# The tiles behind the tail phases of a cross network, multiplied in four 32-column strips instead of one 128-column block

## The chip, the cores and the metric

The kernel runs on one core of a Trainium2 chip. The metric is the time of one execution on the device in microseconds (us). A core has a matrix engine (TensorE; in the profile PE for its matmuls and PEld for its weight loads), VectorE (DVE), ScalarE (ACT), GpSimd (POOL), and SyncE (SP), which issues nearly all transfers here.

## The reference: six cross layers over 16384 rows

```
B, F, D, L = 16384, 26, 16, 6
Din = min(F * D, 1024)                      # 416
x = x0                                      # [16384, 416], bfloat16
for l in range(L):
    proj = jnp.einsum('bd,de->be', x, ws[l]) + bs[l]
    x = x0 * proj + x
return x
```

Each layer is a product of [16384, 416] with [416, 416], a bias, a multiplication with the first input and an addition of the layer's own input.

## The kernel before: groups, jobs, tiles, tails and row products

**Layout.** The 416 features are three full blocks of 128 and a tail of 32. Features stand on partitions and batch rows run along the free dimension, so a weight block is the stationary operand and x the moving one. The batch is cut into 8 groups of 2048 rows, a group into `NJ` = 4 chunks of `CH` = 512, which is one PSUM bank of f32. A job (g, l) is one layer of one group; the list `order` (lines 217 to 221) mixes jobs of several groups so that a layer's inputs are done long before the next layer wants them.

**Tiles.** A job has three tiles, i = 0, 1, 2: 128 output features for all four chunks, in four PSUM banks. `full` (line 467) issues the 12 matmuls over the three full blocks of input features, t = 0, 1, 2, each time for chunks 0 to 3, with 128x128 weights and 512 moving columns (line 479). `rows32` (line 486) adds what the 32 tail features contribute: four matmuls whose weights have 32 rows and 128 columns, each in another strip of 32 array rows (line 500), or, with `small`, sixteen with 32x32 weights (line 494). `evacuate` (line 378) then empties the banks: ScalarE adds the bias (line 406), VectorE multiplies with x0 (line 415) and adds x (line 420).

**Tails.** The 32 output features of the tail would fill a quarter of the array. `tails` (line 506) takes several jobs at once, each with one bank, in which the four chunks lie on the four strips of 32 partitions. It issues per job four 32x32 matmuls for the tail inputs (line 512) and then twelve matmuls with 128x32 weights for the full blocks (line 521): the four chunks of one t are at four column positions of the array, 0, 32, 64 and 96. `evacuate_tail` follows with ScalarE (line 446) and VectorE (lines 448 and 450). There are 14 tail phases: one with a single job at the start, called from `first_job`, and 13 in the list `items`, with 2, 3 or mostly 4 jobs.

**Order.** The program is one list per engine. `Program` works out the semaphore waits from reads and writes; nothing is reordered. PSUM banks are dealt from a ring of eight by `take`. Tiles come in pairs: the first (mode "FR") runs `full`, then `rows32`; the second ("RF") runs `rows32`, then `full`, so that the row products of two tiles stand together. A lone tile ahead of a tail phase has mode "F1": `full`, then the sixteen small row products, behind which the small products of `tails` follow at once. The tile straight behind a tail phase is always the first of a pair, so the array's form goes 32x32, 128x32 (tails), 128x128 (the tile's `full`), 32x128 (row products), 128x128, and so on. The first two tiles of the list have their own function, `two_tiles` (line 812), behind the tail phase of `first_job`: the matmuls of t = 0 for tiles 0 and 1, then t = 1 and 2 for tile 0, the row products of both, and t = 1 and 2 of tile 1.

**A side rule.** In the jobs (1, 2), (2, 1) and (3, 0), `full` splits matmuls into two of 256 columns each until a budget of 63 splits is used up (`HALVES`, `halves`).

**Text of this document.** "Set" is used for the four 128x32 matmuls of one t that stand at the four column positions, and "switch" for a change of the weights' form (rows x columns) from one matmul to the next.

Of the kernel before, what the change touches and what calls it, by code (L numbers as in the profile page):

```python
# [3 lines left out]
P = 128  # L4
CH = 512
T32 = 32
# [15 lines left out]
class Program:  # L22
# [12 lines left out]
    def add(self, eng, fn, reads=(), writes=(), lane=None, batch=None, hold=False, release=False):  # L35
        op = Op(eng, fn, lane, batch)
        deps = {}
        if eng == "pool":
            writes = list(writes) + ["pool"]
        for t in reads:  # L40
            w = self.writer.get(t)
            if w is not None:
                deps[id(w)] = (w, True)
        for t in writes:
            w = self.writer.get(t)
            if w is not None:
                deps[id(w)] = (w, True)
            for r in self.readers.get(t, ()):
                if id(r) not in deps:
                    deps[id(r)] = (r, False)  # L50
        for d, raw in deps.values():
            if d.lane is None and d.eng == eng and lane is None and (eng == "pe" or not raw):
                continue
            op.deps.append(d)
        for t in reads:
            self.readers.setdefault(t, []).append(op)
        for t in writes:
            self.writer[t] = op
            self.readers[t] = []
        if eng == "dve":  # L60
            if hold:
                self.flush()
                self.held = op
            else:
                self.queue[eng].append(op)
                if release:
                    self.flush()
        else:
            self.queue[eng].append(op)
        if lane is not None:  # L70
            batches = self.lanes.setdefault(lane, [])
            if not batches or batches[-1][0] != batch:
                batches.append((batch, []))
            batches[-1][1].append(op)
        return op
# [123 lines left out]
def bass_standalone__cross_network_dcn__recsys_kernel(  # L199
# [8 lines left out]
    NT = 3  # L208
    NJ = 4
# [15 lines left out]
    n = 0  # L225
# [7 lines left out]
    wm = [nc.alloc_sbuf_tensor(f"wm_{l}", [P, NT, D], BF16) for l in range(L)]  # L233
# [14 lines left out]
    psum = nc.alloc_psum_tensor("ps", [P, 8 * CH], FP32)  # L248

    pr = Program(nc)  # L250
    add = pr.add
# [16 lines left out]
    def bank(b, p0=0, p1=P, n=CH):  # L268
        return psum[p0:p1, b * CH:b * CH + n]
# [18 lines left out]
    def wm_tok(l, i):  # L288
        return ("wm", l) if i < 2 else ("wm", l, "rest")
# [58 lines left out]
    def x_src(g, l):  # L348

        if l == 0:  # L350
            s = slot(g)
            return lambda t, a, b: x0s[s][:, t * GC + a * CH:t * GC + b * CH], lambda t, j: x0_tok(s, t, j)
        s = xset[(g, l)]
        return lambda t, a, b: xs[s][:, t * GC + a * CH:t * GC + b * CH], lambda t, j: ("x", s, t, j)
# [109 lines left out]
    HALVES = ((1, 2), (2, 1), (3, 0))  # L464
    halves = [63]

    def full(g, l, i, banks, first, chunk_major, after_chunk=None, chunks=range(NJ), ts_=range(NT)):
        src, stok = x_src(g, l)
        ecols = slice(i * P, (i + 1) * P)
        seq = [(t, j) for j in chunks for t in ts_] if chunk_major else \  # L470
              [(t, j) for t in ts_ for j in chunks]
        for t, j in seq:
            n = 1
            if (g, l) in HALVES and halves[0] and t != (0 if first else NT - 1):
                halves[0] -= 1
                n = 2
            w = CH // n
            for k in range(n):
                add("pe", lambda h, t=t, j=j, k=k, w=w: h.matmul(  # L479
                    bank(banks[j])[:, k * w:(k + 1) * w], wm[l][:, t, ecols], src(t, j, j + 1)[:, k * w:(k + 1) * w],  # L480
                    start=(first and t == 0), stop=(not first and t == NT - 1)),
                    reads=[stok(t, j), wm_tok(l, i)], writes=[("ps", banks[j])])
            if after_chunk and t == NT - 1:
                after_chunk(j)

    def rows32(g, l, i, banks, first, small=False, inner=False):
        src, stok = x3_src(g, l)
        ecols = slice(i * P, (i + 1) * P)
        for j in range(NJ):
            r, q = quad(g, l, j)  # L490
            if small:
                for c in range(NJ):
                    o = slice(c * T32, (c + 1) * T32)
                    add("pe", lambda h, q=q, j=j, r=r, c=c, o=o: h.matmul(  # L494
                        psum[o, banks[j] * CH:(banks[j] + 1) * CH],
                        w3[l][q, i * P + c * T32:i * P + (c + 1) * T32], src[q, :],
                        start=first, stop=not first, tile_position=(r * T32, c * T32)),
                        reads=stok + [("w3", l, r)], writes=[("ps", banks[j])])
                continue
            add("pe", lambda h, q=q, j=j, r=r: h.matmul(  # L500
                bank(banks[j]), w3[l][q, ecols], src[q, :], start=first and not inner,
                stop=not first and not inner,
                tile_position=(r * T32, 0)),
                reads=stok + [("w3", l, r)], writes=[("ps", banks[j])])
# [39 lines left out]
    def load_nat(j, k0, k1):  # L544
# [6 lines left out]
        reads=["warm"], writes=["warm"])  # L551
# [117 lines left out]
    def job_banks():  # L669
        return take(NJ)  # L670
# [41 lines left out]
    def spread(eng):  # L712

        dst = ost[:, :, NT * P:D].rearrange("p (j k) f -> p j k f", j=NJ)
        sp_ = ot3[:, :, :].rearrange("p k (j f) -> p j k f", j=NJ)
        kw = dict(reads=["ot3"], writes=[("ost", NT, j) for j in range(NJ)])
        if eng == "act":
            add("act", lambda h: h.activation(dst, sp_, ACT_F.Copy), **kw)
        else:
            add(eng, lambda h: h.tensor_copy(dst, sp_), **kw)  # L720
# [23 lines left out]
    items = []  # L744
# [35 lines left out]
    def start_job(g, l):  # L780
        started.add((g, l))
        xset[(g, l + 1)] = free_x.pop(0)
        if (g, l) in W_LOAD:
            load_wm(W_LOAD[(g, l)], "sp")
            load_w3(W_LOAD[(g, l)], "sp")
        if (g, l) in G_LOAD:
            load_group(G_LOAD[(g, l)])
# [3 lines left out]
    def finish_tile(g, l, n=1):  # L791
        tiles_done[(g, l)] = tiles_done.get((g, l), 0) + n
        if tiles_done[(g, l)] == NT:
            done_with(g, l)
# [17 lines left out]
    def two_tiles(g, l):  # L812


        assert items[:2] == [("tile", (g, l), 0), ("tile", (g, l), 1)]
        bks = [job_banks(), job_banks()]
        for i in (0, 1):
            full(g, l, i, bks[i], True, False, ts_=[0])
        full(g, l, 0, bks[0], True, False, ts_=[1, 2])
        rows32(g, l, 0, bks[0], False)  # L820
        evacuate(g, l, 0, bks[0], list(range(NJ)), 2)
        finish_tile(g, l)
        rows32(g, l, 1, bks[1], False, inner=True)
        full(g, l, 1, bks[1], False, False, ts_=[1, 2])
        evacuate(g, l, 1, bks[1], list(range(NJ)), 2)
        finish_tile(g, l)
# [3 lines left out]
    for n, it in enumerate(items):  # L830
        if it[0] == "tails":
            tails(it[1])
            continue
        _, (g, l), i = it
        if (g, l) not in started:
            start_job(g, l)
        if n == 0:
            two_tiles(g, l)
            continue
        if n == 1:  # L840
            continue
        if mode[n] in ("FR", "F1"):
            banks = job_banks()
            full(g, l, i, banks, True, False)
            rows32(g, l, i, banks, False, mode[n] == "F1")
            evacuate(g, l, i, banks, list(range(NJ)), 2)
        else:
            banks = job_banks()
            rows32(g, l, i, banks, True)
            if n == len(items) - 1:  # L850
                full(g, l, i, banks, False, True, lambda j: evacuate(g, l, i, banks, [j], 1))
            else:
                full(g, l, i, banks, False, False)
                evacuate(g, l, i, banks, list(range(NJ)), 2)
        finish_tile(g, l)
        if (g, l) == (LAST, L - 2) and i < NT - 1:
            if i:
                spread("act")
            rest_turn(i)


    g, l = LAST, L - 1
    src, stok = x_src(g, l)
# [90 lines left out]
    bks = {0: bka, 1: [b0, b1, b2, a0], 2: [a1, a2, a3, b3], 3: [b0, b1, b2, a0]}  # L954
# [70 lines left out]
```

## Time and profile before

| What | Value |
|---|---|
| Median of 3 runs | 475.86 us (475.6 to 476.08) |
| Span of the profiled execution, first to last instruction | 474.4 us |
| Median less span (what lies around the span) | 1.46 us |
| Granted TensorE clock, mean of the span | 0.999 |
| PE busy; matmuls in the trace | 463.0 us (98%); 3354 |
| Weight loads in the trace | 3408 |
| DVE busy; ACT busy | 404.5 us (85%); 341.2 us (72%) |
| Matmuls of line 521 (tails, 128x32) | 564, 379 to 390 ns each |
| Matmuls of line 479 (full blocks, 128x128) | 1575 with 512 columns, 126 with 256 |

A matmul's duration in this profile is modelled from its issue to the end of its output, and matmuls overlap. The pace of the matrix engine is therefore read from the distance between the starts of neighbours, not from the durations. Some matmul records are missing (3354 of 3408; every matmul has its own weight load, and all the loads are there), so a distance that is longer by exactly one pace is a missing record and no pause. In the timeline view, a line has the start, the time until the last of its instructions ended, the engine, the line of the kernel, the operation with its tiles, the form and the count; what is in brackets is idle time of the engine ahead of it.

### The profile page before, as it was taken

The page shows a single profiled execution, that of the slowest core. Times are in us where ns is not written, and L with a number is a line of the kernel's source. Part 1 is how long each engine was busy: PE and PEld are TensorE (multiplying, and loading weights), DVE is VectorE, ACT ScalarE, POOL GpSimd, SP SyncE. Part 2 cuts the span into 40 slices and gives each one's busy share as a digit, 9 for nine tenths or more (in the row PEclk, how much of TensorE's full clock was granted, in tenths as well). Part 3 has the DMA queues.
Part 4 walks back from the last instruction along what each step waited for, and adds up shares of the span by engine and source line. Part 5 has one row for each costly group of instructions (what it writes and reads, how often), then busy time and mean ns, then how long its engine had stood idle before and what let it go on. Part 6 is the DMA issues. An engine that isn't in the chain of part 4 may idle for free.

```text
span 474.4 us, 8414 instructions
## 1 busy us (share of the span) xinstructions
PE 463.0 (98%) x3354; PEld 200.0 (42%) x3408; DVE 404.5 (85%) x700; ACT 341.2 (72%) x371; POOL 6.6 (1%) x15
## 2 busy tenths in 40 slices
PE   8999999999999999999999999999999999999996
PEld 5344444654444444444444444444444444444442
DVE  1888888888888888898889869988888888888897
ACT  4687777777777777777777777777777777777775
POOL 1000000000000000000000000000000000001000
PEclk9999999999999999999999999999999999999999
DMA  8996830730102388369319950880001039026999
GB/s 224 183 176 142 177 84 1 137 87 1 33 2 46 69 234 145 76 146 233 89 24 163 245 102 7 191 271 1 1 10 27 0 62 240 22 46 102 234 166 289
DMA packets 139052, 53.18 MB, mean 112 GB/s; under 512 B 112763, under 2 KB 138501, under 8 KB 139013
## 3 DMA queue, kind: packets, MB, share of 16 engines
q1 hardware_dynamic: 138856, 52.54, 50.0%
q8 instruction: 26, 0.43, 0.4%
q10 hardware_dynamic: 156, 0.11, 0.1%
q14 instruction: 14, 0.11, 0.1%
HBM read 5.97 MB, written 13.63 MB: 41 GB/s over the span
## 4 chain that ended last, share of the span: by engine, by line
PE 92%; DMA 2%; DVE 2%; ACT 2%; issue 1%; SPq 0%; DVEq 0%
PE ps L479 77%; PE ps L500 7%; PE ps L521 6%; ACT tw L406 2%; DMA wm<-in_ws_dram 1%; PE ps L494 1%; DVE x L940 1%; DMA x<-x 1%; DVE x L934 1%; PE ps L512 1%; DMA ot<-x 1%; DVE tw L415 0%; PE ps L600 0%; SPq L545 0%; DVE x L610 0%
## 5 line engine op out<-in xcount | busy, mean ns | idle before, releaser
L406 ACT ACTIVATE tw<-ps,bias 128x1024 bf16<-128x1024 f32 (+1 forms) x295 | 299.8, 1071 | 119.5 <-PE ps L500 81.1
L479 PE MATMUL ps<-x,wm 128*128 128x512 bf16 (+1 forms) x1701 | 372.1, 371 | 6.2 <-issue 3.7
L479 PEld LDWEIGHTS ps<-x,wm 128*128 128x128 bf16 x1755 | 165.1, 98 | 209.5 <-issue 28.2
L415 DVE TENSOR_TENSOR tw<-tw,x 128x1024 bf16<-128x1024 bf16 (+1 forms) x285 | 192.6, 683 | 51.9 <-ACT tw L406 51.5
L420 DVE TENSOR_TENSOR x<-tw,x 128x1024 bf16<-128x1024 bf16 (+1 forms) x285 | 182.5, 681 | 0.0
L500 PE MATMUL ps<-x,w 32*128 32x512 bf16 x512 | 39.2, 379 | 0.0
L521 PE MATMUL ps<-x,wm 128*32 128x512 bf16 x564 | 33.0, 380 | 0.0
L446 ACT ACTIVATE ts<-ps,bias 128x512 bf16<-128x512 f32 x47 | 28.8, 701 | 0.0
L450 DVE TENSOR_TENSOR x<-ts,x 128x512 bf16<-128x512 bf16 x47 | 18.6, 417 | 3.9 <-DMA x<-x 3.9
L521 PEld LDWEIGHTS ps<-x,wm 128*32 128x32 bf16 x564 | 13.8, 96 | 17.6 <-issue 5.3
L500 PEld LDWEIGHTS ps<-x,w 32*128 32x128 bf16 x512 | 7.8, 92 | 26.9 <-issue 26.4
L448 DVE TENSOR_TENSOR ts<-ts,x 128x512 bf16<-128x512 bf16 x47 | 18.6, 418 | 0.0
L720 POOL COPY ost<-ot 128x512 bf16<-128x512 bf16 x6 | 5.1, 854 | 422.2 <-DMA ot<-x 422.2
L876 PE MATMUL ps<-wm,x 128*128 128x416 bf16 x48 | 9.7, 340 | 0.0
L610 DVE COPY x<-ps 128x512 bf16<-128x512 bf16 x5 | 2.0, 423 | 8.9 <-PE ps L600 8.9
L928 ACT ACTIVATE x<-ps 128x416 bf16<-128x416 f32 x16 | 7.7, 517 | 2.1 <-PE ps L876 1.9
L612 ACT ACTIVATE x<-ps 128x512 bf16<-128x512 bf16 x7 | 3.8, 595 | 5.6 <-PE ps L600 5.6
L876 PEld LDWEIGHTS ps<-wm,x 128*128 128x128 bf16 x48 | 4.2, 98 | 4.4 <-issue 1.0
L512 PE MATMUL ps<-x,w 32*32 32x512 bf16 x188 | 5.9, 374 | 0.0
L494 PE MATMUL ps<-x,w 32*32 32x512 bf16 x208 | 5.6, 385 | 0.0
L940 DVE TENSOR_TENSOR x<-x,x 128x832 bf16<-128x832 bf16 (+1 forms) x9 | 4.7, 541 | 0.2
L934 DVE TENSOR_TENSOR x<-x,x 128x832 bf16<-128x832 bf16 (+1 forms) x10 | 4.8, 498 | 0.0
(40 smaller groups left out, 34.0 us busy)
## 6 DMA issues: line engine op xcount, KB each, us to landing
out_dram<-ost SPq DMA_DIRECT2D x6, 1664.0 KB, 7.0
x<-x SPq DMA_DIRECT2D x24, 96.0 KB, 2.1
x<-in_x_dram SPq DMA_DIRECT2D x8, 208.0 KB, 4.9
x<-in_x_dram SPq DMA_DIRECT2D x4, 416.0 KB, 8.4
out_dram<-ost SPq DMA_DIRECT2D x2, 832.0 KB, 5.5
wm<-in_ws_dram SPq DMA_DIRECT2D x5, 312.0 KB, 3.5
x<-x SPq DMA_DIRECT2D x22, 64.0 KB, 2.0
out_dram<-x SPq DMA_DIRECT2D x3, 416.0 KB, 4.4
```

The source lines that it names most:

```text
L406: add("act", lambda h, a=a, w=w, b0=b0: h.activation(tw[r][:, a * CH:(a + w) * CH], psum[:, b0 * CH:(b0 + w) * CH], ACT_F.Identity, bias=b ...
L415: add("dve", lambda h, a=a, e=e: h.tensor_tensor(tw[r][:, a * CH:e * CH], tw[r][:, a * CH:e * CH], x0s[s0][:, i * GC + a * CH:i * GC + e * ...
L420: add("dve", lambda h, a=a, e=e: h.tensor_tensor(xs[so][:, i * GC + a * CH:i * GC + e * CH], tw[r][:, a * CH:e * CH], src(i, a, e), ALU.ad ...
L446: add("act", lambda h: h.activation(ts[r][:, :], bank(b), ACT_F.Identity, bias=bias[:, 3, l:l + 1], scale=1.0), reads=[("ps", b), "bias"], ...
L448: add("dve", lambda h: h.tensor_tensor(ts[r][:, :], ts[r][:, :], x03, ALU.mult), reads=[("ts", r)] + tok0, writes=[("ts", r)], release=True)
L450: add("dve", lambda h: h.tensor_tensor(x3s[so][:, :], ts[r][:, :], res, ALU.add), reads=[("ts", r)] + rtok, writes=[("x3", so), ("x3", so, ...
L479: add("pe", lambda h, t=t, j=j, k=k, w=w: h.matmul(bank(banks[j])[:, k * w:(k + 1) * w], wm[l][:, t, ecols], src(t, j, j + 1)[:, k * w:(k ...
L494: add("pe", lambda h, q=q, j=j, r=r, c=c, o=o: h.matmul(psum[o, banks[j] * CH:(banks[j] + 1) * CH], w3[l][q, i * P + c * T32:i * P + (c + ...
L500: add("pe", lambda h, q=q, j=j, r=r: h.matmul(bank(banks[j]), w3[l][q, ecols], src[q, :], start=first and not inner, stop=not first and no ...
L512: add("pe", lambda h, l=l, b=b, s3=s3, ri=ri, qi=qi, ro=ro, qo=qo: h.matmul(psum[qo, b * CH:(b + 1) * CH], w3[l][qi, NT * P:D], s3[qi, :], ...
L521: add("pe", lambda h, t=t, j=j, src=src, l=l, b=b, ro=ro, qo=qo: h.matmul(psum[qo, b * CH:(b + 1) * CH], wm[l][:, t, NT * P:D], src(t, j, ...
L876: add("pe", lambda h, t=t: h.matmul(bank(b, n=D), xcol(t, j, kk), wm[l][:, t, :], start=(first and t == 0), stop=(not first and t == NT - 1)),
```

## The change

`full` gets a flag `columns`. With it, each 128x128 matmul becomes four matmuls with 128x32 weights, at column positions 0, 32, 64 and 96, which write the four strips of 32 partitions of the same bank and read the same 128x512 piece of x. The flag is set for every tile of mode "FR" or "F1" that follows a tail phase in the list, and in `two_tiles` for what stands ahead of the row products. The row products of these tiles, and all other tiles, stay as they are. The split into halves is passed over for a tile with the flag.

```diff
-    def full(g, l, i, banks, first, chunk_major, after_chunk=None, chunks=range(NJ), ts_=range(NT)):
+    def full(g, l, i, banks, first, chunk_major, after_chunk=None, chunks=range(NJ), ts_=range(NT), columns=False):
...
         for t, j in seq:
+            if columns:
+                for c in range(NJ):
+                    o = slice(c * T32, (c + 1) * T32)
+                    add("pe", lambda h, t=t, j=j, c=c, o=o: h.matmul(
+                        psum[o, banks[j] * CH:(banks[j] + 1) * CH],
+                        wm[l][:, t, i * P + c * T32:i * P + (c + 1) * T32], src(t, j, j + 1),
+                        start=(first and t == 0), stop=(not first and t == NT - 1), tile_position=(0, c * T32)),
+                        reads=[stok(t, j), wm_tok(l, i)], writes=[("ps", banks[j])])
+                continue
             n = 1
...
         for i in (0, 1):
-            full(g, l, i, bks[i], True, False, ts_=[0])
-        full(g, l, 0, bks[0], True, False, ts_=[1, 2])
+            full(g, l, i, bks[i], True, False, ts_=[0], columns=True)
+        full(g, l, 0, bks[0], True, False, ts_=[1, 2], columns=True)
...
             banks = job_banks()
-            full(g, l, i, banks, True, False)
+            full(g, l, i, banks, True, False, columns=items[n - 1][0] == "tails")
             rows32(g, l, i, banks, False, mode[n] == "F1")
```

Thirteen tiles of the list get 36 matmuls and 36 weight loads more each, and `two_tiles` gets 48 of each more.

## The prediction, on record before the run

> **What bounds the kernel now.** I read the page first, then the groups with their forms kept apart, then the timeline around one tail phase in ever narrower windows.
>
> ```profile
> span 474.4 us, 8414 instructions
> PE 463.0 (98%) x3354; PEld 200.0 (42%) x3408; DVE 404.5 (85%) x700; ACT 341.2 (72%) x371; POOL 6.6 (1%) x15
> ...
> PEclk9999999999999999999999999999999999999999
> ...
> PE 92%; DMA 2%; DVE 2%; ACT 2%; issue 1%; SPq 0%; DVEq 0%
> ```
>
> PE holds 92% of the chain that ended last and its clock is whole throughout, so time taken off PE's own list of work comes off the end, unless a wait takes its place. A busy share says nothing about the pace, so I look at starts. The groups with forms apart give what a narrow and a wide weight load cost:
>
> ```profile
> L479 PEld LDWEIGHTS ps<-x,wm 128*128 128x128 bf16 x1755 | 165.1, 98 | 209.5 <-issue 28.2 <-ACT ts L446 3.8 <-ACT bias L643 1.1
> L521 PE MATMUL ps<-x,wm 128*32 128x512 bf16 x564 | 33.0, 380 | 0.0
> L521 PEld LDWEIGHTS ps<-x,wm 128*32 128x32 bf16 x564 | 13.8, 96 | 17.6 <-issue 5.3
> ```
>
> One load takes 96 to 98 ns in either form. The timeline around the tail phase at 155 us (four jobs), one window wide:
>
> ```profile
> 154.68 0.43 PE L494 MATMUL ps<-x,w 32*32 32x512 bf16 x16
> 154.90 0.42 PE L512 MATMUL ps<-x,w 32*32 32x512 bf16 x16
> 155.22 2.12 ACT L406 ACTIVATE tw<-ps,bias 128x1024 bf16<-128x1024 f32 x2 [1.27 <-PE ps L494]
> 155.26 2.77 PE L521 MATMUL ps<-x,wm 128*32 128x512 bf16 x48
> 157.22 2.42 ACT L446 ACTIVATE ts<-ps,bias 128x512 bf16<-128x512 f32 x4
> 157.96 2.27 PEld L479 LDWEIGHTS ps<-x,wm 128*128 128x128 bf16 x12 [0.42 <-ACT ts L446]
> 158.19 2.54 PE L479 MATMUL ps<-x,wm 128*128 128x512 bf16 x11 [0.16 <-issue]
> 160.66 0.61 PE L500 MATMUL ps<-x,w 32*128 32x512 bf16 x8
> ```
>
> and in narrow windows, where single starts can be seen:
>
> ```profile
> 155.49 0.60 PE L521 MATMUL ps<-x,wm 128*32 128x512 bf16 x8
> ...
> 157.64 0.39 PE L521 MATMUL ps<-x,wm 128*32 128x512 bf16 x4
> ...
> 160.35 0.38 PE L479 MATMUL ps<-x,wm 128*128 128x512 bf16 x1
> ```
>
> The reader is to see three things. **The pace:** the second set of four starts at 155.49 and the twelfth at 157.64: ten steps in 2.15 us, 0.216 a set. Single 128x128 matmuls run at the same pace: from 158.19 to 160.35 there are ten steps, 2.16 us. So four narrow matmuls side by side cost what one wide one costs. **The switch:** from the tails' last set (157.64) to the first wide matmul, whose record is missing (12 loads, 11 matmuls; its load starts at 157.96), it is 0.32 and not 0.216. From the last wide matmul (160.35) to the first row product (160.66) it is 0.31. From a switch's first matmul or set to the second it is again some 0.01 more than the pace (158.19 less 157.96 is 0.23). So a switch costs 0.09 to 0.12 us, each way and between all the forms here. **Nobody waits:** between 154.68 and 160.66 PE has no other gap.
>
> **The change, part by part.**
>
> 1. *The switch behind the tails goes.* Before, the last set of the tails to the first row product: 160.66 - 157.64 = 3.02 us. After, twelve more sets follow at the pace, 12 x 0.216 = 2.59, and then the switch from a set of four to 32x128. That last step isn't in the trace. Nearest rows: 0.31 for wide to 32x128 (160.35 to 160.66), measured from a single matmul; 0.32 for a set of four to wide; 0.35 for a block of sixteen 32x32 to a set of four (154.90 to 155.26). I take 0.32, the same set on its way out. After: 2.59 + 0.32 = 2.91; gain 0.11 us a tile. With 0.31 it is 0.12, with 0.35 it is 0.08. The switch ahead of the row products stays, so one of two goes.
>
> 2. *How often.* 13 tiles of the list, all behind tails and ahead of 32x128 row products, and the same in `two_tiles`, where the tails' last set starts at 18.77 and the wide matmul at 19.09: 0.32 again. There tiles 0 and 1 are both in the narrow form until the rows; tile 1 goes on in the wide form behind them, as before. 14 x 0.11 = 1.5 us; by the bounds 14 x 0.08 = 1.1 to 14 x 0.12 = 1.7.
>
> 3. *Four matmuls instead of one.* 13 x 36 + 48 = 516 more matmuls and as many loads, at nothing if they run side by side as the tails do. One thing differs: in a tail set, the four stream four chunks of x; here all four stream one and the same piece with four weight strips. The nearest row is L494: sixteen 32x32 matmuls, four to a stream, with 0.22 us from their start to the start of the next sixteen (154.68 to 154.90). Sharing a stream doesn't serialise them there. If it did here, a tile would take 48 x 0.216 = 10.4 us instead of 2.6; that row is my reason to leave this out of the range. The four write four strips of one bank, as in the tails. Nothing new is on the semaphores: the row products behind still end the tile.
>
> A rule speaks against it: in the Trainium skill, "TensorEngine Tiling (Array Packing)", section "Gotcha 2: Feature Incompatibilities", column tiling excludes fast weight load. By that rule the loads should become the limit; by this trace a 32-column load takes 96 ns against 98, and the tails' sets keep the pace, so I put no term for it.
>
> 4. *Issue.* The dense stretch grows from 80 matmuls (16 + 16 + 48, with as many loads) to 128. PE must be fed 4 matmuls in 0.216 us, 54 ns each, for twice as long. In the tails it was: 80 in the 2.96 us from 154.68 to 157.64 with no gap. How many had been lined up during the wide tile ahead, the trace doesn't show. If all 32 small ones had, the other 48 came in 2.96 us, so at least one in 62 ns; that is the slowest feed that this trace allows. If none had, it is one in 37. Over the longer stretch, from 154.68 to the last column set at 160.23, 96 in 5.55 us would do, one in 58. So only a feed between 58 and 62 ns, or a smaller reserve with a feed slower than 54, hurts.
>
> The Trainium skill, "TensorE: Matmul & The Clock Gate", section "Wait — 56ns, not 53.3ns?", states some 62 ns a matmul when its decoding isn't done in hardware. By that figure a narrow tile would take 48 x 62 = 2.98 us and not 2.59 once the reserve is used up; no run here shows which decoding is on.
>
> 5. *Instructions to fetch.* 1032 more. The page's instruction queue had 26 packets for PE's 6762 loads and matmuls, so some 260 a packet: 4 more packets. None of the 26 made a gap on PE, and the dense stretch of 256 instructions lasts about as long as one packet's worth. I put nothing.
>
> 6. *What a PE that arrives 0.11 us earlier meets.* The tile behind the tails uses banks that ACT empties at L406. At 155 us ACT ends at 157.34, and the bank's first load was at 158.19: 0.85 us to spare. With three jobs (52 us) ACT's three evacuations end at 52.51 and the load was at 52.87: 0.36. In `two_tiles` ACT's L446 ends at 20.21 and the load is at 20.40: 0.19. All over 0.11, so nothing becomes late; if that cover were gone, only the 0.11 of that place would be lost. VectorE follows ACT, which follows PE. The split budget of 63 is still used up, by the next tile of those jobs. The last 20 us (transposes, stores, natural-order products) start from PE's results and move with it.
>
> **Sum.** 1.5 us off the profiled span, 474.4 to 472.9. What lies around the span (475.86 - 474.4 = 1.46) isn't touched, so 475.86 - 1.5 = **474.4 us**, 0.3% faster. A difference under about 0.2% (0.95 us) can't be told from no change in a measurement of this kernel.
>
> **Rivals.**
>
> - *The pace of the new sets is a little slower, and the gain is eaten.* In the chain of waits, twelve pairs of load and transpose that come one after the other (L600 at 10.67) take 0.67 us, 56 ns each; if a narrow pair could be had only every 56 ns, a set takes 0.224: 12 x 0.008 = 0.1 us a tile, all of the gain. Time about 475.8. Against it: the tails' sets at 0.216. For it: the tails may live on a reserve. Chance 0.11.
> - *Slower: the feed.* If PE gets a matmul only every 62 ns, the bound from part 4, and the reserve is spent in the tails, a tile takes 2.98 instead of 2.59: +0.39 less 0.11 is +0.28, by 13 tiles +3.6: 479.5. It decides from 56 ns on (2.59 + 0.11 over 48). It would show as steps over 0.216 in the second half of the narrow tile. Against it: it needs reserve and feed to fail together just behind what the trace shows. Chance 0.09.
> - *The change doesn't do what it says*, a switch remains since PE treats tail sets and column sets as two forms, though both are 128x32: 475.9. Counted with the first rival; nothing in the trace speaks for it, since a tail set goes to the next job's bank and weights without a step.
>
> **Numbers.** Gain as reckoned 0.80, eaten or absent 0.11, slower 0.09. The likeliest case alone runs from 474.2 to 474.8 (1.7 and 1.1 off). For 8 in 10 I go down by the runs' own spread (0.24) to 473.9 and reach up through the eaten gain to 475.8; what is left out is the slow feed and little else. Faster 0.80, same 0.11, slower 0.09.
>
> **What would show it.** Right: no step above 0.216 between the tails' last set and the first column set; twelve sets in 2.59 us; 0.32 to the row products; PE's span to the row products 2.91; ACT's L406 behind these tiles 0.11 earlier, phase by phase up to 1.5 at the end. Wrong: sets at 0.22 or more, growing late in the tile (feed); a gap at an instruction packet; the first load of a bank later than ACT's end by only a few hundredths (a bank); or PE 1.5 us ahead at 450 us and the end not (the transfers at the end).

## The result and the profile after

The changed kernel takes 474.33 us (median of 6 runs, 473.85 to 474.74), the kernel before took 475.97 us beside it (6 runs, 475.17 to 476.1). The ratio is 0.9972, 95% interval 0.9962 to 0.9981: 1.64 us less by the medians (0.9 to 1.8 by the interval), against 1.5 forecast. Two single executions among the experiments below lie far from the rest (one of one_more, 688.88 us, and one of one_more_45, 1697.29 us); they move the medians given there by 0.03 us at most.

From the page of the changed kernel, the span, the busy times and the chain by engine:

```profile
span 472.6 us, 9500 instructions
...
PE 467.1 (99%) x3924; PEld 202.9 (43%) x3924; DVE 404.3 (86%) x700; ACT 341.2 (72%) x371; POOL 6.3 (1%) x15
...
PE 95%; DVE 3%; ACT 1%; DMA 1%; issue 0%; DVEq 0%
```

PE is still the bound; the counts are up by the 516 loads. (All matmul records are there this time.) The lines of the code have moved by up to 9: L479 is now L488 in the wide form and L476 in the narrow form, L494 is L503, L500 is L509, L512 is L521 and L521 is L530. The groups with forms apart:

```profile
L488 PEld LDWEIGHTS ps<-x,wm 128*128 128x128 bf16 x1583 | 149.4, 98 | 185.7 <-issue 26.9 <-ACT x L621 0.6 <-DVE tw L415 0.4
L476 PE MATMUL ps<-x,wm 128*32 128x512 bf16 x688 | 39.5, 379 | 0.0
L476 PEld LDWEIGHTS ps<-x,wm 128*32 128x32 bf16 x688 | 18.4, 97 | 18.7
```

688 narrow matmuls, in 39.5 us of busy time (14.3 tiles of 12 wide matmuls at 0.216 us would be 37.2, and the last output of each stretch comes on top), each load 97 ns. The tail phase that was shown before is now at 154 us. Its timeline, in one window and then in narrow ones:

```profile
154.15 2.77 PE L530 MATMUL ps<-x,wm 128*32 128x512 bf16 x48
...
156.54 2.48 PEld L476 LDWEIGHTS ps<-x,wm 128*32 128x32 bf16 x48
156.75 2.76 PE L476 MATMUL ps<-x,wm 128*32 128x512 bf16 x48
...
159.45 0.61 PE L509 MATMUL ps<-x,w 32*128 32x512 bf16 x8
```

```profile
156.54 0.39 PE L530 MATMUL ps<-x,wm 128*32 128x512 bf16 x4
156.75 0.39 PE L476 MATMUL ps<-x,wm 128*32 128x512 bf16 x4
159.13 0.39 PE L476 MATMUL ps<-x,wm 128*32 128x512 bf16 x4
159.45 0.39 PE L509 MATMUL ps<-x,w 32*128 32x512 bf16 x4
```

The tails' last set starts at 156.54 and the first column set at 156.75: one pace and no switch; its first load is already at 156.54, under the set ahead, where before it came 0.32 us after that set's start. The twelfth column set starts at 159.13 (eleven steps in 2.38 us, 0.216 each), and 0.32 us later the row products. From the tails' last set to the rows: 2.91 us, as forecast; before 3.02.

**Not all of the span's 1.8 us is the change.** The first wide matmuls of the profiled executions, before and after:

```profile
6.55 1.46 PE L479 MATMUL ps<-x,wm 128*128 128x512 bf16 x6 [0.53 <-DMA wm<-in_ws_dram]
```

```profile
5.81 1.60 PE L488 MATMUL ps<-x,wm 128*128 128x512 bf16 x6
```

In that execution of the kernel before, the first weights landed later. Its time wasn't the median either: in the runs listed, the time is 1.75 to 2.08 us more than the span of the same execution, so a span of 474.4 goes with some 476.2 us, above the 475.97. At the first tail phase, ahead of any edit, the changed kernel's execution is 0.57 us earlier. From there the lead grows at each phase: 0.57, 0.68, 0.79, 0.89, 1.00, 1.11 and so on to 1.96 at the fourteenth, and 2.07 after the last treated tile. That is 14 steps, together 1.49 us (1.39 us in the 13 steps from the first phase to the fourteenth), 0.107 each. The tails of the first and of the fourteenth phase, before and after:

```profile
18.33 0.83 PE L521 MATMUL ps<-x,wm 128*32 128x512 bf16 x12
...
447.29 1.48 PE L521 MATMUL ps<-x,wm 128*32 128x512 bf16 x24
```

```profile
17.75 0.83 PE L530 MATMUL ps<-x,wm 128*32 128x512 bf16 x12
...
445.33 1.48 PE L530 MATMUL ps<-x,wm 128*32 128x512 bf16 x24
```

Behind the last treated tile some is lost again (2.07 down to 1.79), most of it between the last vector instruction and the end; more on that below.

### The profile page after: what moved, and what is told of

It is laid out like the page before. It is cut to its first block, busy times and chain, and to the rows that moved or that the text cites. A ratio compares the mean times of both kernels' runs of the same rounds, so it can differ in the third digit from the quotient of the medians.

```text
span 472.6 us, 9500 instructions
## 1 busy us (share of the span) xinstructions
PE 467.1 (99%) x3924; PEld 202.9 (43%) x3924; DVE 404.3 (86%) x700; ACT 341.2 (72%) x371; POOL 6.3 (1%) x15
## 4 chain that ended last, share of the span: by engine, by line
PE 95%; DVE 3%; ACT 1%; DMA 1%; issue 0%; DVEq 0%
PE ps L488 70%; PE ps L476 8%; PE ps L509 7%; PE ps L530 7%; PE ps L503 1%; DVE x L949 1%; DVE x L943 1%; PE ps L591 1%; PE ps L609 1%; ACT tw L406 1%; PE ps L521 1%; DMA ot<-x 1%; DVE tw L415 0%; DVE x L420 0%; DVE x L905 0%
## 5 line engine op out<-in xcount | busy, mean ns | idle before, releaser
L488 PE MATMUL ps<-x,wm 128*128 128x512 bf16 (+1 forms) x1583 | 340.2, 371 | 0.0
L488 PEld LDWEIGHTS ps<-x,wm 128*128 128x128 bf16 x1583 | 149.4, 98 | 185.7 <-issue 26.9
L476 PE MATMUL ps<-x,wm 128*32 128x512 bf16 x688 | 39.5, 379 | 0.0
L509 PE MATMUL ps<-x,w 32*128 32x512 bf16 x512 | 39.2, 379 | 0.0
L530 PE MATMUL ps<-x,wm 128*32 128x512 bf16 x564 | 33.0, 380 | 0.0
L476 PEld LDWEIGHTS ps<-x,wm 128*32 128x32 bf16 x688 | 18.4, 97 | 18.7
L530 PEld LDWEIGHTS ps<-x,wm 128*32 128x32 bf16 x564 | 13.8, 96 | 17.6 <-issue 5.3
L509 PEld LDWEIGHTS ps<-x,w 32*128 32x128 bf16 x512 | 7.8, 92 | 27.0 <-issue 26.5
L521 PE MATMUL ps<-x,w 32*32 32x512 bf16 x188 | 5.9, 374 | 0.0
L503 PE MATMUL ps<-x,w 32*32 32x512 bf16 x208 | 5.7, 385 | 0.0
```

What stands on the lines that cost most here:

```text
L476: add("pe", lambda h, t=t, j=j, c=c, o=o: h.matmul(psum[o, banks[j] * CH:(banks[j] + 1) * CH], wm[l][:, t, i * P + c * T32:i * P + (c + 1) ...
L488: add("pe", lambda h, t=t, j=j, k=k, w=w: h.matmul(bank(banks[j])[:, k * w:(k + 1) * w], wm[l][:, t, ecols], src(t, j, j + 1)[:, k * w:(k ...
L509: add("pe", lambda h, q=q, j=j, r=r: h.matmul(bank(banks[j]), w3[l][q, ecols], src[q, :], start=first and not inner, stop=not first and no ...
L521: add("pe", lambda h, l=l, b=b, s3=s3, ri=ri, qi=qi, ro=ro, qo=qo: h.matmul(psum[qo, b * CH:(b + 1) * CH], w3[l][qi, NT * P:D], s3[qi, :], ...
L530: add("pe", lambda h, t=t, j=j, src=src, l=l, b=b, ro=ro, qo=qo: h.matmul(psum[qo, b * CH:(b + 1) * CH], wm[l][:, t, NT * P:D], src(t, j, ...
```

## The experiments

Theory: a change of the weights' form costs PE 0.107 us, wherever it stands, and the change takes 14 away. Rivals: the narrow form itself or the place of its instructions makes the gain; the feed of narrow matmuls is near its bound; only some kinds of switch cost.

All times are medians, with the kernel before measured beside them. Leads and gains between tail phases are worked out from the starts of the tails' first loads in the two traces.

### late_switch: the switch put back, eight sets later

```diff
-            if columns:
+            if columns and t < NT - 1:
```

> Narrow sets for t = 0 and 1 only; t = 2 of the tiles behind the tails is wide again. Nearly as many narrow matmuls as in the changed kernel, but the switch that was removed comes back, eight sets later. Theory (each switch costs 0.107 us, wherever it stands): all of the gain goes, time within 0.2 us of the kernel before (0 instead of -1.6), and in the trace the tail phases lie 0.00 us apart from those of before once the start is taken off. Rival A (the gain comes from the narrow form itself, or from where its instructions fall): two thirds or more of the gain stay, -1.0 us or better.

476.01 against 475.48 us, ratio 1.0011 (1.0001 to 1.0020). The tile that ends in wide matmuls, from its timeline:

```profile
157.16 1.90 PE L476 MATMUL ps<-x,wm 128*32 128x512 bf16 x32
159.22 0.81 PE L488 MATMUL ps<-x,wm 128*128 128x512 bf16 x3 [0.16 <-issue]
159.96 0.39 PE L509 MATMUL ps<-x,w 32*128 32x512 bf16 x4
```

The pause is back, now ahead of t = 2 (one record is missing, so three of four matmuls are seen). The distance to the kernel before is 0.70 us at the first tail phase, 0.70 at each of the others and 0.70 at the last: the gain is gone to the hundredth, with two thirds of the narrow matmuls still there. Rival A falls. But the time is 0.5 us above before where 0 was expected, and the trace puts that behind PE's last phases. I could not explain it at this point.

### all_narrow: every tile of the list but the last in narrow sets

```diff
-            full(g, l, i, banks, True, False, columns=items[n - 1][0] == "tails")
+            full(g, l, i, banks, True, False, columns=True)
...
-                full(g, l, i, banks, False, False)
+                full(g, l, i, banks, False, False, columns=True)
```

Tile 1 in `two_tiles` is narrow throughout as well.

> Every tile of the list but the last is multiplied in narrow sets: 8277 matmuls instead of 3924, and as many switches as in the changed kernel. Theory (four narrow matmuls cost one wide one, and the feed holds): as the changed kernel, -1.6 us against before, within 0.4 (the split into halves falls away too, 63 x 2.5 ns = 0.16 us off). Rival B (the feed lives on a reserve): at one matmul in 58 ns a tile of 48 costs 0.2 us more, by some 120 tiles +24 us; at one in 62 ns 0.39 us, +47 us. Rival C (the 4 times as many instructions come late from memory): gaps on the matrix engine of about 1 us at the instruction packets, some 34 packets more, up to +30 us.

474.65 against 475.48 us, 0.9981 (0.9972 to 0.9991): -0.8. Its groups:

```profile
L476 PE MATMUL ps<-x,wm 128*32 128x512 bf16 x6576 | 368.6, 379 | 0.0
...
L476 PEld LDWEIGHTS ps<-x,wm 128*32 128x32 bf16 x6576 | 170.3, 97 | 191.6 <-issue 25.9 <-DVE tw L415 0.4 <-ACT tw L406 0.2
```

6576 narrow matmuls without a slow one among them: 64 instruction packets and no gap on PE. From one block of row products to the next it is 5.837 us for two tiles, against 5.829 with wide ones: 8 ns, since the fourth matmul of a set starts 10 ns after the first and the switch counts from there. Rivals B (+24 us or more) and C fall. Some 50 pairs of tiles at 8 ns each are 0.4 us, less 0.16 for the splits that fell away: from the first to the last tail phase the gain is 1.09 us where the changed kernel's is 1.39. That is part of the way from the expected -1.6 to -0.8; more goes behind the last tail phase (below).

### narrow_256: the feed at twice the rate

```diff
-                for c in range(NJ):
+                m = 2 if t else 1
+                w = CH // m
+                for k, c in [(k, c) for k in range(m) for c in range(NJ)]:
...
-                        psum[o, banks[j] * CH:(banks[j] + 1) * CH],
-                        wm[l][:, t, i * P + c * T32:i * P + (c + 1) * T32], src(t, j, j + 1),
+                        psum[o, banks[j] * CH + k * w:banks[j] * CH + (k + 1) * w],
+                        wm[l][:, t, i * P + c * T32:i * P + (c + 1) * T32], src(t, j, j + 1)[:, k * w:(k + 1) * w],
```

> In the flagged tiles the narrow matmuls of t = 1 and 2 are split in two of 256 columns: 64 of them and 16 with 512 columns per tile, 27 ns for each if the pace holds (half of 0.216 us and a few ns for four). Theory with a feed that is never near its bound: 14 x 16 more steps of a few ns, +0.3 us on top of the changed kernel, -1.2 us against before. Rival B (a feed of one matmul in 54 ns is near the bound): at one in 40 ns a tile takes 0.8 us more, by 14 +11 us on top of the changed kernel; at one in 54 ns 1.7 us more, +24 us.

475.27 against 475.44 us, 1.0000 (0.9991 to 1.0009). The treated tile in its timeline:

```profile
156.75 2.78 PE L478 MATMUL ps<-x,wm 128*32 128x512 bf16 x80
159.46 0.61 PE L511 MATMUL ps<-x,w 32*128 32x512 bf16 x8
```

(The form given for the 80 is the first one's; 64 have 256 columns.) 156.75 to 159.46 is 2.71 us against 2.70 in the changed kernel. The sets of 256 start every 0.109 us, 27 ns a matmul with its load, so a feed of one in 54 is half of what PE was seen to take over a stretch of 64. Rival B, which wanted 0.8 us more a tile or worse, falls. On PE the cost is 0.020 us a tile, 0.28 in all, as expected. In the time, 1 us more is missing, and again it is lost at the very end.

### more_switches: 122 switches added

```diff
-            if columns:
+            if columns and (first or t == 1):
...
-                full(g, l, i, banks, False, False)
+                full(g, l, i, banks, False, False, columns=True)
```

> The changed kernel, and besides in the 61 tiles that begin with the row products the four matmuls of t = 1 are narrow sets between wide matmuls of t = 0 and 2: two switches more in each, 122 in all, and no other work. Theory: 122 x 0.107 = 13.0 us on top of the changed kernel, +11.4 us against before. Rival A (switches are free and something else made the gain): -1.6 us. Rival D (only the switch out of the narrow form costs): half, +4.9 us.

488.0 against 475.48 us, 1.0263 (1.0248 to 1.0279): +12.5. One of these tiles in the timeline:

```profile
164.01 0.81 PE L488 MATMUL ps<-x,wm 128*128 128x512 bf16 x3 [0.16 <-issue]
164.75 1.05 PE L476 MATMUL ps<-x,wm 128*32 128x512 bf16 x16
165.73 2.55 PE L488 MATMUL ps<-x,wm 128*128 128x512 bf16 x11
```

Between the first and the last tail phase this kernel loses 11.78 us on the kernel before although it has the change's 13 gains there (1.39): 120 of the 122 switches stand in between, and 13.17 by 120 is 0.110 us a switch. Rivals A and D fall, and the price holds in both directions.

### strips_64: strips of 64 columns

```diff
-                for c in range(NJ):
-                    o = slice(c * T32, (c + 1) * T32)
+                for c in range(2):
+                    o = slice(c * 64, (c + 1) * 64)
```

The weights' slices and tile positions follow.

> The flagged tiles in two strips of 64 columns instead of four of 32. Theory in its strict form (any change of the weights' form is a switch): the tails' 128x32 to 128x64 is a switch again, so the time of before, 0 within 0.2 us. Rival E (only the way between a whole array and strips costs): the gain stays, -1.6 us. In the trace: the step from the tails' last set to the first pair of 64 is 0.32 us or 0.216 us.

476.17 against 475.48 us, 1.0013 (1.0004 to 1.0023). Its timeline:

```profile
154.84 2.77 PE L530 MATMUL ps<-x,wm 128*32 128x512 bf16 x48
157.54 2.78 PE L476 MATMUL ps<-x,wm 128*64 128x512 bf16 x24
160.26 0.61 PE L509 MATMUL ps<-x,w 32*128 32x512 bf16 x8
```

From the tails' first set to the first pair of 64 it is 2.70 us, against 2.60 to the first column set in the changed kernel (154.15 to 156.75): a switch. So it isn't enough to be in strips; the form must be the same. The Trainium skill says so in "TensorEngine Tiling (Array Packing)", section "Key Properties": changing the tiling mode, not just the tile, drains the engine. The trace agrees: the change of form costs 0.107 us, and the four positions of one set start within 10 ns. On PE this kernel falls 0.013 us a phase behind the one before; in the time 0.7 us, and the rest is at the end once more.

### every_second: a dose

The narrow form behind every second phase of the list, by a counter in the condition of `columns`.

> The narrow form behind every second tail phase of the list only (7 of 13) and in the first two tiles: 8 switches fewer than before instead of 14. Theory: -0.86 us, and in the trace the distance to before grows by 0.107 us at each treated phase and by nothing at the others. Rival A (the place of the instructions, or the start): no steps of this kind, or all of the gain at once.

475.73 against 475.44 us, 1.0005 (0.9996 to 1.0015). The leads over before at the tail phases are 0.70, 0.81, 0.92, 0.92, 1.02, 1.02, 1.13, 1.13 and so on to 1.45: a step of 0.107 at each treated phase and none at the others. The trace is the theory's; the time isn't: 0.3 us slower and not 0.86 faster.

### one_more: one more switch, in the first job

```diff
-        full(g, l, 0, ba, True, True, chunks=[2, 3])
+        full(g, l, 0, ba, True, True, chunks=[2, 3], columns=True)
```

> The changed kernel, and in the first job the six matmuls of tile 0, chunks 2 and 3, which follow the tails' transposes in the 128x32 form, are narrow too: one switch fewer. Theory: 0.107 us less between the transposes and the first tail phase in the trace, -0.1 us in the time, which can't be told apart. Rival F (at the start the matrix engine waits for its operands, so a switch there is hidden): 0.00 us between them in the trace.

475.19 against 475.44 us, 0.9995 (0.9985 to 1.0004). From the transposes to the first tails it is 6.760 us, against 6.735. So rival F holds: there is nothing to gain where PE waits for its operands. And the time has lost 1 us against the changed kernel, which ran beside it at 474.18.

### Where the microsecond at the end comes from

Six kernels by now were 0.5 to 1.3 us slower than their phases said (late_switch, more_switches, strips_64, narrow_256, every_second, one_more). In all of them most of it goes between the last vector instruction and the end. The changed kernel ran once more, as after_again, beside narrow_256, every_second and one_more, and has nothing of this:

> The changed kernel once more, on the chip of the next three runs. Theory: -1.5 us against before, by 14 switches of 0.107 us, 0.107 at each tail phase in the trace; the first measurement said -1.6 (0.9972).

474.18 against 475.44 us, 0.9974 (0.9963 to 0.9984). The issues of the last store with their time to landing (last column, us), first in after_again, then in one_more, each with its instruction queue:

```profile
q8 instruction: 30, 0.49, 0.4%
...
out_dram<-x ACTq DMA_DIRECT2D x1, 104.0 KB, 2.2
```

```profile
q8 instruction: 31, 0.51, 0.4%
...
out_dram<-x ACTq DMA_DIRECT2D x1, 104.0 KB, 3.3
```

(In the first profile of the changed kernel the same store took 2.5 us, so 0.3 us here is spread.) In one_more there is one instruction packet more, of 16 KB, which took 0.89 us and by the packet records started 3.6 us before the last vector instruction ended, among the closing stores. Half-microsecond stretches in which the stores end, in the changed kernel and in one_more (DMA share and GB/s are the last two columns):

```profile
471.00:471.50 0.50, 0.00 (x0) 0.00 (x0) 0.00 (x0) 0.00 (x0) 0.00 (x0) 0.50 0.17 42
471.50:472.00 0.50, 0.00 (x0) 0.00 (x0) 0.00 (x0) 0.00 (x0) 0.00 (x0) 0.50 0.01 2
```

```profile
470.50:471.00 0.50, 0.00 (x0) 0.00 (x0) 0.00 (x0) 0.00 (x0) 0.00 (x0) 0.50 0.33 98
471.00:471.50 0.50, 0.00 (x0) 0.00 (x0) 0.00 (x0) 0.00 (x0) 0.00 (x0) 0.50 0.07 22
471.50:472.00 0.50, 0.00 (x0) 0.00 (x0) 0.00 (x0) 0.00 (x0) 0.00 (x0) 0.50 0.07 20
```

In the changed kernel the share falls to nothing at once. In one_more it stays at 0.07 for a microsecond: that is the share of about one of the 16 DMA engines, late by about the time of that packet. Before that the engines have no pause in which one could catch up: in each 2 us from 460 to 470 us the share is 1.08 or more in both kernels (over 1, since the times of packets overlap). New theory: PE's instructions come in packets of 16 KB (7848 loads and matmuls by 30 packets are 262 each, all_narrow's 16554 by 64 are 259; I take 256 a packet); the length of PE's list decides where the last ones fall; and one among the closing stores costs up to 1 us.

| Kernel | PE loads and matmuls modulo 256 | Gain from the first to the 14th tail phase | Last instruction packet, us before the last vector instruction's end | From there to the end of the span (the closing), us |
|---|---|---|---|---|
| before | 160 | - | 19.4 | 2.84 |
| changed | 168 | 1.39 | 19.6 | 3.03 |
| after_again | 168 | 1.39 | 19.6 | 2.76 |
| late_switch | 88 | 0.00 | 11.1 | 3.33 |
| more_switches | 66 | -11.78 | 10.1 | 3.42 |
| narrow_256 | 40 | 1.13 | 8.7 | 3.82 |
| every_second | 248 | 0.75 | 5.6 | 3.48 |
| strips_64 | 248 | -0.18 | 5.3 | 3.52 |
| one_more | 204 | 1.39 | 3.6 | 3.82 |
| all_narrow | 170 | 1.09 | 18.4 | 2.25 |

The closing overstates the loss. Between the last tail phase and the last vector instruction, the six kernels of the first sentence are 0.1 to 0.4 us shorter than the one before; from the last tail phase to the end their traces lose 0.25 (late_switch) to 0.64 us (narrow_256). The medians lack more than that, and one trace of each kernel doesn't show the rest.

The length can be set without touching a switch: each split of the side rule is one load and one matmul more, at 2.5 ns of pace. So three kernels with another budget, and one to look for a better place.

**one_more_45**

```diff
-    halves = [63]
+    halves = [45]
```

on one_more.

> As one_more, with the budget of splits at 45 instead of 63: 18 matmuls and 18 loads fewer, so that the matrix engine's list is as long as the changed kernel's again (3924 of each). Fetch theory (one_more loses about 1 us at the end since a 31st instruction packet of 16 KB comes 3.6 us before the last vector instruction, among the closing stores): 30 packets, the last 19.5 us before that, the closing store lands in 2.2 us instead of 3.3, time -1.6 us against before and not -0.25. Rival (the narrow matmuls of the first job cost it, in some way that I don't see): the time stays at -0.25, whatever the packets do.

474.11 against 475.52 us, 0.9972 (0.9961 to 0.9983), beside 0.9995 for one_more: the microsecond is back, with the narrow matmuls of the first job unchanged. 30 packets by its page; the 1697.29 us execution is the profiled one, so no other figure is read from its trace, and it has no row in the table.

**after_81**: budget 81 in the changed kernel, with job (0, 4) added to `HALVES` so that there is enough to split.

> The changed kernel with 18 splits more (budget 81, and job (0, 4) among those that split): no switch is added or taken, the list has 3942 matmuls, as one_more's. The splits cost 18 x 2.5 ns = 0.05 us by the pace. Fetch theory: a 31st instruction packet among the closing stores, the last one lands 1.1 us later, time -0.4 us against before instead of -1.6. Rival (length doesn't matter): -1.5 us.

475.07 against 475.52 us, 0.9993 (0.9984 to 1.0002): most of the gain gone by 18 splits. 31 packets, the last 3.6 us ahead; from the last vector instruction to the end 3.83 us. The phases' gain is 1.34, of 1.39.

**every_second_23**: budget 23 in every_second.

> As every_second, with the budget at 23 instead of 63: 40 matmuls fewer, the list is four packets' worth (3 x 256 instructions, to within a few) from that of the kernel before... that is, its length modulo 256 is the changed kernel's. Fetch theory with the switch theory: no packet among the closing stores, and the 8 switches removed (0.86 us) and 40 splits (0.1 us) show in the time: -0.9 to -1.0 us against before, instead of +0.15. Rival: it stays within 0.3 us of before.

474.68 against 475.52 us, 0.9985 (0.9976 to 0.9993): -0.84 where every_second had +0.3 and -0.9 to -1.0 was expected. Last packet 19.6 us ahead, 2.75 us to the end, phases 0.85 (0.75 and 40 splits at 2.5 ns). The dose now shows in the time as well.

**one_more_26**: budget 26 in one_more.

> As one_more, with the budget at 26: the length modulo 256 is 130, between those whose last packet came 11 us (88) and 19.5 us (160) before the last vector instruction, so about 15.5 us before it. Two effects against each other: kernels whose last packet is not at 19.5 us began the last section some 0.3 us earlier, and those with it at 11 us or later closed 0.5 to 1 us later. If the packet at 15.5 us disturbs neither, -2.0 us against before; if it still delays the stores, -1.2 to -1.5 us.

474.66 against 475.52 us, 0.9982 (0.9973 to 0.9991): -0.9, a miss. The last packet was 17.0 us ahead and the closing took 2.25 us, the shortest. But between the last tail phase and the last vector instruction this kernel lost 0.86 us, all_narrow (18.4 us ahead, closing 2.25 as well) 0.50. So a packet there costs ahead of the stores what it saves in them. The chains that ended last show the transfer, a DMA transpose whose result ScalarE and then VectorE wait for; its lines in the changed kernel, one_more_26 and all_narrow:

```profile
452.62 2.51 DMA ot<-x
```

```profile
451.34 4.59 DMA ot<-x
```

```profile
452.43 3.63 DMA ot<-x
```

In one_more_26 the last packet starts at 453.34 us, within this transpose, and in all_narrow at 452.13, just ahead of it; in the changed kernel it is over before (450.03). Counted from the fourteenth tail phase, the transpose lands 0.89 us later than in the changed kernel in one_more_26 and 0.52 us later in all_narrow, about the whole loss of the section. That the packet is the reason is argued from this overlap; no run moves the packet alone. After_81 and one_more, with packets at the same places, differ by 0.3 us in this section; that stays open. No version was found that beats the changed kernel beyond the measurement: one_more_45's ratio is the same 0.9972.

## Why the prediction was right

- *Part 1, the switch.* 0.11 us a tile was forecast from 3.02 us before and 2.91 after, with the assumed 0.32 on the way to the row products. Measured: 0.107, 2.91 us from the last tail set to the rows, 0.32 on the way out. The bounds of 0.08 and 0.12 weren't needed.
- *Part 2, how often.* 14 steps of 0.107, 1.49 us, one at each phase; late_switch takes all of them back, every_second has the half that it should.
- *Part 3, side by side.* Column sets on one and the same stream run at 0.216 us. The row with sixteen 32x32 matmuls was the right neighbour. The rule on fast weight loads, weighed there, shows in no time here: 97 ns a load, under the set ahead.
- *Part 4, the feed.* No bound in sight: 54 ns a matmul over the list in all_narrow, 27 ns in narrow_256. The 62 ns a matmul of the Trainium skill ("TensorE: Matmul & The Clock Gate", section "Wait — 56ns, not 53.3ns?") is its case without hardware decoding; 54 ns held over all of all_narrow's list says that it isn't the case here. The reserve of the tails, on which two rivals stood, isn't needed.
- *Part 5, instructions.* The count was right (30 packets instead of 26), and nothing was lost. The reason given was not enough. I looked for gaps on PE, of which there are none even with 64 packets; the cost of a packet is in another place, a late store. That the change keeps its gain hangs on a coincidence: it adds 1032 instructions, 4 x 256 + 8, so its last packet falls where it fell before. With 36 more, after_81, it measured -0.45 us, within the bound of no change. So the mechanism was right, but that the whole gain came through to the time was luck, and so is the hit to 0.07 us: beside 29 runs of the kernel before, after_again gave 1.26 us and not 1.64.
- *Part 6, who is met.* The three margins went as worked out: 0.85, 0.36 and 0.19 us became 0.74, 0.25 and 0.08. In the first two tiles, one more gain of this size would have met ScalarE. That the last 20 us move with PE held for this kernel (0.03 us from the last tail phase to the last vector instruction) and not for others (one_more_26 lost 0.86 there).
- *The sum.* The 1.46 us around the span was a median less the span of another execution; 1.75 to 2.08 us is what the runs show. The forecast doesn't lean on it, since it takes 1.5 off the median.
- *The rivals.* Eaten gain and slow feed both needed a slower pace of the sets; it isn't there. That tail sets and column sets might count as two forms is refuted by the step of one pace between them, and strips_64 shows what it would have looked like.

## What to carry to other kernels

On a PE-bound list, count the changes of the weights' form (rows by columns) along the list, not only the matmuls; each is a fixed price in this kernel, and a stretch can be given its neighbour's form at next to no cost on PE (8 ns for two tiles), here with strips that fill the array. Take the gain only where PE isn't waiting for operands. For differences of a microsecond, split the time into its start, the phases, and the closing behind the last vector instruction before believing a median: an edit that alters an instruction list's length can move an instruction packet into the last stores.

## What the runs showed of the hardware that wasn't expected

- Instruction packets of 16 KB, 0.9 to 1.8 us each, share the DMA engines with the kernel's stores. One that starts 3.6 to 11 us before the last vector instruction ends goes with a closing of 3.3 to 3.8 us instead of 2.8 to 3.0; 17.0 and 18.4 us ahead it is 2.25. That the list's length decides over the microsecond is shown by lists of equal switches and other lengths (one_more against one_more_45, the changed kernel against after_81); that it does so by the place of the last packet is read from the table, not tested apart. How a packet holds up a store that is issued 3 us and more after it is argued only: the engines have no pause in between (a share of 1.08 or more), so one that is behind stays behind.
- PE takes a narrow matmul and its load every 27 ns (256 columns, four strips) over stretches of 64, with no sign of a bound; longer stretches at this pace weren't run.
- The price of a switch doesn't depend on which sides change: from the start of the last matmul of one form to the first of the next it is 0.31 us for rows (128x128 to 32x128), columns (128x32 to 128x128) and both (128x32 to 32x128), 0.09 more than the pace, and 0.01 more follows it.
